# V caches loaded in 32 KB runs with a lag of three steps, no closing barrier, and a smaller last load, in a decode kernel with cached attention

## Chip, cores, metric

One core of a Trainium2 chip. The metric is the device time of the kernel in microseconds (us), median of several executions. TensorE is called PE, VectorE DVE, ScalarE ACT; SP is the engine that issues the loads. A load has landed when the last of the 16 DMA engines that share it has reported. Its forerunner is the load ahead of it in the queue. The lead of a load is the time from its issue to the landing of its forerunner.

## The reference

One token goes through a transformer block: layer norm and modulation, attention over a cache of 65,536 keys (32 query heads, 4 KV heads, head size 128), output projection, layer norm again, and a gated GELU feed-forward layer (1024 to 3584 to 1024).

```python
mod = (_silu(c) @ w_mod).reshape(c.shape[0], 6, 1, -1)      # six vectors sa, ca, ga, sb, cb, gb
h = _layernorm(x) * (1 + ca) + sa
q = (h @ wq) per head;  k, v = k_cache, v_cache repeated 8 times
p = _softmax(q k^T * Dh ** -0.5);  o = p v
x = x + ga * (o @ wo)
h = _layernorm(x) * (1 + cb) + sb
x = x + gb * ((_gelu(h @ w_gate) * (h @ w_up)) @ w_down)
```

K and V are 67.1 MB each, the weights 51.4 MB: 185.6 MB are read for one token. The rest of the work is small.

## The kernel before

The caches are cut into NC = 32 chunks of 8192 keys: 2 MB of K and 2 MB of V each, 64 keys (16 KB) on each of the 128 partitions. SBUF holds ten slots of 2 MB. K uses slots 0 to 3 and comes in pairs of chunks (4 MB, 32 KB a partition); V uses slots 4 to 7 and comes chunk by chunk (2 MB, 16 KB a partition).

```python
SITES = 4
KU = 2
# ... planning: the order of the queue of loads
for i in range(NC + 2):
    if i < NC and i % KU == 0:
        j_k[i] = plan_load(kv_src(kh, i, KU), flat(KU * CH, DH), i % SITES, kfill[i % SITES // KU], KU)
    if i >= 2:
        j = i - 2
        j_v[j] = plan_load(kv_src(vh, j), flat(CH, DH), SITES + j % SITES, vfill[j % SITES])
# ... then the weights: wo (4 loads), gate (4), up (4), down (3 of 2 MB, then 2 of 512 KB)
```

SP issues the loads strictly in this order. Each waits until PE has finished with what lay in its slots:

```python
def issue_ready():
    while issued[0] < len(loads):
        j = loads[issued[0]]
        if any(q.freed is None for q in j.prev):
            return
        SP.wait(*(q.freed for q in j.prev))
        sp.dma_start(j.view, j.src).then_inc(j.tok[0], 16)
        issued[0] += 1
```

PE works in steps. Step i transposes K chunk i (T), multiplies Q by K chunk i-1 (QK) and P by V chunk i-2 (PV), interleaved in quarters. MT and MB are small matmuls for the maxima of the scores. DVE and ACT copy the transposes out, take the maxima and make the exponentials.

```python
def PV(q):
    j = i - 2
    # ...
    if q == 0:
        pwait(vfill[s], j, it)      # V has landed
        pwait(ex[s], j, it)         # its exponentials are made
    # ... 16 matmuls with V as the stationary operand
    if q == NB - 1:
        release(j_v[j], pt[("PV", j)])

T(0); QK(0); T(1); QK(1); PV(0); T(2); QK(2); QK(3); PV(1); T(3); PV(2); MT(); PV(3); MB()   # shown on one line
```

Steps 0 to 3 are written out; steps 4 to 31 are a loop of four steps in PE's program; steps 32 to 34 and all that follows are written out again. Everything stands in a block whose end is a barrier of all engines:

```python
with nc.Block() as block:
    @block.sync
    def _(sp_unused):
        emit_all()
```

## Time and profile before

443.58 us (443.48 to 443.66, three runs).

| read from the profile | value |
|---|---|
| span of the profiled execution | 441.8 us (its time: 443.68) |
| PE busy | 333.3 us, 75% |
| DMA, mean over the span | 421 GB/s |
| K pair (4 MB), landing to landing, median | 9.67 us |
| V chunk (2 MB), landing to landing, median | 4.85 us |
| last landing; end of span | 438.37; 441.80 us |

The last V chunk was issued at 344.54 and the load ahead of it landed at 361.04, so SP was 16.5 us early.

### The profile page before, as it was taken

The numbers are of one execution on the slowest core, as the hardware profiler recorded it, in microseconds if no ns is written. First come the engines' busy times: TensorE is split into PE (matmuls) and PEld (weight loads), VectorE is DVE, ScalarE is ACT, GpSimd is POOL, SyncE is SP. The second block draws the span as 40 slices with busy tenths as digits, with TensorE's granted clock in tenths as the row PEclk, the third lists the DMA queues.
The fourth block names the chain that finished last, engine by engine and source line by source line (L and its number), as shares of the span: only waits on it lengthen the run. The fifth ranks groups of instructions, "written<-read, shape, count | busy, mean of one in ns | idle before, by whom it ended". The sixth has DMA issues, their size and how long they took to land.

```text
span 441.8 us, 16747 instructions
## 1 busy us (share of the span) xinstructions
PE 333.3 (75%) x7849; PEld 323.6 (73%) x7849; DVE 164.9 (37%) x282; ACT 142.9 (32%) x548; POOL 3.7 (1%) x21
## 2 busy tenths in 40 slices
PE   1333428889998987988898899979998797367534
PEld 1332427879988987988898899879998796367434
DVE  1000006534645564365446336534545343401000
ACT  1000003643434563435246343524643344200000
POOL 2000000000000000000000000000000000000000
PEclk9999999965968998599669759956969758555555
DMA  8999999999999999999999999999999999999994
GB/s 330 425 426 426 449 429 418 444 412 436 427 423 444 418 445 416 442 433 424 438 426 447 421 438 425 433 442 421 437 423 445 426 429 429 422 424 425 424 425 182
DMA packets 13088, 186.08 MB, mean 421 GB/s; under 512 B 1280, under 2 KB 1280, under 8 KB 3584
## 3 DMA queue, kind: packets, MB, share of 16 engines
q1 hardware_dynamic: 13024, 185.60, 98.4%
q8 instruction: 25, 0.41, 0.3%
q14 instruction: 7, 0.06, 0.0%
q10 hardware_dynamic: 32, 0.00, 0.0%
HBM read 185.60 MB, written 0.00 MB: 420 GB/s over the span
## 4 chain that ended last, share of the span: by engine, by line
DMA 53%; PE 40%; issue 3%; ACT 2%; DVE 1%; SPq 1%
DMA slots<-in_A_v_cache_dram 27%; PE kt_ps L419 22%; DMA slots<-in_A_k_cache_dram 9%; PE b L483 8%; PE sc_ps L439 7%; DMA slots<-in_B_w_up_dram 6%; DMA slots<-in_B_w_down_dram 6%; DMA slots<-in_w_mod_dram 5%; PE b L463 2%; ACT p_sb L549 1%; SPq L216 1%; ACT kt_sb L518 1%; PE b L453 1%; PE kt_ps L318 0%; DVE kt_sb L518 0%
## 5 line engine op out<-in xcount | busy, mean ns | idle before, releaser
L419 PE MATMUL kt_ps<-ident,slots 128*128 128x128 bf16 x2048 | 171.4, 251 | 18.7 <-DMA slots<-in_A_k_cache_dram 15.9
L419 PEld LDWEIGHTS kt_ps<-ident,slots 128*128 128x128 bf16 x2048 | 147.8, 114 | 20.5 <-issue 10.2
L518 DVE COPY kt_sb<-kt_ps 128x2048 bf16<-128x2048 bf16 x96 | 117.5, 1224 | 108.2 <-PE kt_ps L419 108.0
L518 ACT ACTIVATE kt_sb<-kt_ps 128x2048 bf16<-128x2048 bf16 x32 | 60.1, 1877 | 224.7 <-PE kt_ps L419 224.7
L483 PE MATMUL b<-p_sb,slots 128*128 128x8 bf16 x2048 | 70.4, 167 | 22.2 <-DMA slots<-in_A_v_cache_dram 9.6
L549 ACT ACTIVATE p_sb<-sc_ps,mneg 128x64 bf16<-128x64 f32 x256 | 83.5, 561 | 5.0 <-DVE mneg L544 5.0
L483 PEld LDWEIGHTS b<-p_sb,slots 128*128 128x128 bf16 x2048 | 64.7, 99 | 24.8 <-issue 13.5
L549 ACT ACTIVATION_READ_ACCUMULATOR p_sb<-sc_ps,mneg 128x1 f32 x256 | 77.1, 366 | 0.0
L439 PE MATMUL sc_ps<-q_buf,kt_sb 128*128 128x8 bf16 x2048 | 67.4, 167 | 1.1 <-issue 1.1
L439 PEld LDWEIGHTS sc_ps<-q_buf,kt_sb 128*128 128x128 bf16 x2048 | 65.3, 100 | 1.2 <-issue 1.1
L537 DVE TENSOR_REDUCE m_col<-sc_ps 128x8 f32<-128x512 f32 x32 | 21.8, 681 | 5.2 <-PE sc_ps L439 5.2
L318 PE MATMUL kt_ps<-h_col,slots 128*128 128x1 bf16 x448 | 16.0, 172 | 10.0 <-DMA slots<-in_B_w_up_dram 7.0
L318 PE MATMUL sc_ps<-s_col,slots 128*128 128x1 bf16 x384 | 11.5, 165 | 15.8 <-DMA slots<-in_w_mod_dram 15.8
L318 PEld LDWEIGHTS kt_ps<-h_col,slots 128*128 128x128 bf16 x448 | 15.5, 118 | 10.5 <-DMA slots<-in_B_w_up_dram 7.4
L318 PEld LDWEIGHTS sc_ps<-s_col,slots 128*128 128x128 bf16 x384 | 11.1, 105 | 16.4 <-DMA slots<-in_w_mod_dram 16.4
L542 DVE TENSOR_REDUCE mg<-b 8x1 f32<-8x128 f32 x32 | 8.9, 279 | 32.5 <-PE b L453 32.5
L318 PE MATMUL sc_ps<-h_col,slots 128*128 128x1 bf16 x256 | 7.4, 165 | 12.6 <-DMA slots<-in_A_wq_dram 12.6
L318 PEld LDWEIGHTS sc_ps<-h_col,slots 128*128 128x128 bf16 x256 | 7.1, 104 | 12.9 <-DMA slots<-in_A_wq_dram 9.3
L463 PE MATMUL b<-negi,mg 8*128 8x8 f32 x64 | 14.3, 294 | 0.4 <-DVE mg L542 0.4
L318 PE MATMUL kt_ps<-u_col,slots 128*128 128x1 bf16 x224 | 6.6, 165 | 9.3 <-DMA slots<-in_B_w_down_dram 9.3
L463 PEld LDWEIGHTS b<-negi,mg 8*128 8x128 f32 x64 | 11.4, 220 | 2.7 <-DVE mg L542 0.6
L318 PEld LDWEIGHTS kt_ps<-u_col,slots 128*128 128x128 bf16 x224 | 6.3, 104 | 9.6 <-DMA slots<-in_B_w_down_dram 6.4
(74 smaller groups left out, 62.5 us busy)
## 6 DMA issues: line engine op xcount, KB each, us to landing
slots<-in_A_k_cache_dram SPq DMA_DIRECT2D x16, 4096.0 KB, 19.4
slots<-in_A_v_cache_dram SPq DMA_DIRECT2D x32, 2048.0 KB, 26.7
slots<-in_w_mod_dram SPq DMA_DIRECT2D x8, 1536.0 KB, 19.0
slots<-in_A_wq_dram SPq DMA_DIRECT2D x4, 2048.0 KB, 37.1
slots<-in_A_wo_dram SPq DMA_DIRECT2D x4, 2048.0 KB, 33.1
slots<-in_B_w_gate_dram SPq DMA_DIRECT2D x4, 1792.0 KB, 30.0
slots<-in_B_w_up_dram SPq DMA_DIRECT2D x4, 1792.0 KB, 28.9
slots<-in_B_w_down_dram SPq DMA_DIRECT2D x3, 2048.0 KB, 30.3
```

Of the source, the lines that this page charges most:

```text
L216: sp.dma_start(j.view, j.src).then_inc(j.tok[0], 16)
L318: ins = pe.matmul(bank[:, j:j + 1], w, rhs[:, k0 + kk:k0 + kk + 1], start=first, stop=True, skip_group_check=True,)
L419: ins = pe.transpose(kt_ps[:, half * 2048 + t * P:half * 2048 + (t + 1) * P], j_k[i - i % KU].view[:, i % KU * CH + b * TB + t, :], ident[ ...
L439: ins = pe.matmul(sc_ps[:, base + n * REP:base + (n + 1) * REP], kt_sb[:, j % 2, n, :], q_buf[:, j % SITES, :], start=True, stop=True,)
L453: ins = pe.transpose(b6[0:REP, 32:32 + P], m_col[:, j % 2, :], identf[:, :]) if emit else None
L463: ins = pe.matmul(b6[:, 256:256 + REP], mg8[:, j % 2:j % 2 + 1].to_broadcast([REP, P]), negi[:, :], start=True, stop=True,)
L483: ins = pe.matmul(b7[:, s * REP:(s + 1) * REP], j_v[j].view[:, n, :], p_sb[:, s, n, :], start=(n == 0), stop=(n == CH - 1),)
L518: ev[i % SITES][b].done(act.activation(dst, src, ACT.Copy) if E_ is AC else dve.tensor_copy(dst, src))
L537: m1[s].done(dve.tensor_reduce(m_col[:, j % 2, :].unsqueeze(2), scv, AX.X, ALU.max))
L542: m2[s].done(dve.tensor_reduce(mg8[:, j % 2:j % 2 + 1], b6[0:REP, 32:32 + P], AX.X, ALU.max))
L549: ins = act.activation(p_sb[:, s, :, h], scv[:, h, :], ACT.Exp, bias=mneg[:, j, h:h + 1], scale=scale, accum_out=z_all[:, j, h:h + 1],)
```

## The change

The intent: V, like K, in runs of 32 KB a partition, so half as many packets; hence two V buffers of 4 MB instead of four of 2 MB. PV is put a third step behind T, so that PE does not stand waiting for a pair. The closing barrier goes, since SP waits for the output anyway. The last down load is halved, so that fewer matmuls follow the last landing.

The core of the diff (renamings and formatting cut):

```diff
-KU = 2
+UN = 2
+LAG = 3
@@ load planning @@
-        for i in range(NC + 2):
-            if i < NC and i % KU == 0:
-                j_k[i] = plan_load(kv_src(kh, i, KU), ...)
-            if i >= 2:
-                j = i - 2
-                j_v[j] = plan_load(kv_src(vh, j), flat(CH, DH), SITES + j % SITES, vfill[j % SITES])
+        for i in range(0, NC + UN, UN):
+            if i < NC:
+                j_k[i] = plan_load(kv_src(kh, i, UN), ...)
+            if i >= UN:
+                j = i - UN
+                j_v[j] = plan_load(
+                    kv_src(vh, j, UN), flat(UN * CH, DH), SITES + j % SITES, vfill[j % SITES // UN], UN)
@@ last block of w_down @@
-            for e in range(0, UE, 2):
-                jb = plan_load(wd_v[:, b, e:e + 2, :], flat(2, D), next(tail))
+            for e, ne in ((0, 2), (2, 1), (3, 1)):
+                jb = plan_load(wd_v[:, b, e:e + ne, :], flat(ne, D), next(tail))
@@ QK @@
+                if b == 0 and j >= 2:
+                    pwait(ex[(j - 2) % SITES], j - 2, it)
@@ PV @@
-                j = i - 2
+                j = i - LAG
-                    pwait(vfill[s], j, it)
-                    pwait(ex[s], j, it)
+                    if j % UN == 0:
+                        pwait(vfill[s // UN], j, it)
+                    if i > NC:
+                        pwait(ex[s], j, it)
-                    release(j_v[j], pt[("PV", j)])
+                    release(j_v[j - j % UN], pt[("PV", j)], j % UN)
@@ end @@
-    with nc.Block() as block:
-
-        @block.sync
-        def _(sp_unused):
-            emit_all()
-
+    emit_all()
```

(The cut parts let each half of a pair be freed by itself. A load is issued when both halves of what lay there before are free.)

More of the change, by code (lines that the diff above doesn't have):

```diff
@@ L182, in bass_adaLN_cond__gqa_block_cached__geglu_ffn__decode_kernel @@
     nfill = [0] * NSLOT
-    kfill = [Site(nc, f"kfill{i}", 16) for i in range(SITES // KU)]
-    vfill = [Site(nc, f"vfill{i}", 16) for i in range(SITES)]
+    kfill = [Site(nc, f"kfill{i}", 16) for i in range(SITES // UN)]
+    vfill = [Site(nc, f"vfill{i}", 16) for i in range(SITES // UN)]
     last_job = [None] * NSLOT
@@ L197, in plan_load @@
         job.src = src
-        job.freed = None
+        job.freed = [None] * nslot
         job.prev = []
-        for t in range(slot, slot + nslot):
-            if last_job[t] is not None and last_job[t] not in job.prev:
-                job.prev.append(last_job[t])
-            last_job[t] = job
+        for t in range(nslot):
+            if last_job[slot + t] is not None:
+                job.prev.append(last_job[slot + t])
+            last_job[slot + t] = (job, t)
         loads.append(job)
@@ L212, in issue_ready @@
             j = loads[issued[0]]
-            if any(q.freed is None for q in j.prev):
+            if any(q.freed[t] is None for q, t in j.prev):
                 return
-            SP.wait(*(q.freed for q in j.prev))
+            SP.wait(*(q.freed[t] for q, t in j.prev))
             sp.dma_start(j.view, j.src).then_inc(j.tok[0], 16)
@@ L219, in bass_adaLN_cond__gqa_block_cached__geglu_ffn__decode_kernel, with release @@
     in_loop = [False]
-    def release(job, tok):
-        job.freed = tok
+    def release(job, tok, part=0):
+        job.freed[part] = tok
         if not in_loop[0]:
@@ L249, in emit_all @@
         j_k, j_v = {}, {}
-        for i in range(NC + 2):
-            if i < NC and i % KU == 0:
-                j_k[i] = plan_load(kv_src(kh, i, KU), flat(KU * CH, DH), i % SITES, kfill[i % SITES // KU], KU)
-            if i >= 2:
-                j = i - 2
-                j_v[j] = plan_load(kv_src(vh, j), flat(CH, DH), SITES + j % SITES, vfill[j % SITES])
+        for i in range(0, NC + UN, UN):
+            if i < NC:
+                j_k[i] = plan_load(kv_src(kh, i, UN), flat(UN * CH, DH), i % SITES, kfill[i % SITES // UN], UN)
+            if i >= UN:
+                j = i - UN
+                j_v[j] = plan_load(
+                    kv_src(vh, j, UN), flat(UN * CH, DH), SITES + j % SITES, vfill[j % SITES // UN], UN)
         tail = iter([8, 9, 0, 1, 2, 4, 3, 5, 6, 7, 8, 9] + [0, 1, 2, 4, 3, 5, 6, 7])
@@ L271, in emit_all @@
         while b < NBF:
-            for e in range(0, UE, 2):
-                jb = plan_load(wd_v[:, b, e:e + 2, :], flat(2, D), next(tail))
-                j_d.append((jb, jb.view, b * UE + e, 2))
+            for e, ne in ((0, 2), (2, 1), (3, 1)):
+                jb = plan_load(wd_v[:, b, e:e + ne, :], flat(ne, D), next(tail))
+                j_d.append((jb, jb.view, b * UE + e, ne))
             b += 1
@@ L409, in T @@
                 s, half = i % SITES, b % 2
-                if b == 0 and i % KU == 0:
-                    pwait(kfill[s // KU], i, it)
+                if b == 0 and i % UN == 0:
+                    pwait(kfill[s // UN], i, it)
                 if b >= 2:
@@ L420, in T @@
                             kt_ps[:, half * 2048 + t * P:half * 2048 + (t + 1) * P],
-                            j_k[i - i % KU].view[:, i % KU * CH + b * TB + t, :],
+                            j_k[i - i % UN].view[:, i % UN * CH + b * TB + t, :],
                             ident[:, :],
@@ L424, in T @@
                 pt[("T", i, b)] = PE.done(ins)
-                if b == NB - 1 and i % KU == KU - 1:
-                    release(j_k[i - i % KU], pt[("T", i, b)])
+                if b == NB - 1:
+                    release(j_k[i - i % UN], pt[("T", i, b)], i % UN)
             def QK(b):
@@ L483, in PV @@
                         ins = pe.matmul(
-                            b7[:, s * REP:(s + 1) * REP], j_v[j].view[:, n, :], p_sb[:, s, n, :],
+                            b7[:, s * REP:(s + 1) * REP], j_v[j - j % UN].view[:, j % UN * CH + n, :], p_sb[:, s, n, :],
                             start=(n == 0), stop=(n == CH - 1),
@@ L520, in OC @@
             def OC():
-                j = i - 3
+                j = i - LAG - 1
                 if not 0 <= j < NC:
@@ L577, in emit_all @@
         mode[0] = "emit"
-        for i in range(LAST, NC + 3):
+        for i in range(LAST, NC + LAG + 1):
             pe_step(i)
```

## The prediction

> **What bounds the kernel now.** The DMA engines. The slices show them at 9 tenths or more from the second to the last but one; the page gives 421 GB/s on average. The trace's packets leave no idle time: from about 10 to 430 us at least 16 are always in flight, one for each engine. The Trainium skill ("DMA: Bandwidth & Descriptors", "Where 436 GB/s comes from") puts the ceiling at 435.2 GB/s; K at 9.67 us for 4 MB (landing to landing, from the DMA issues) is 434 GB/s, so this trace agrees. PE is busy 75% and waits: for K 15.9 us, for V 9.6 us, for P's exponentials 3.6 us plus 9 us "issue" (table of waits). Its clock is halved about half the time; a step takes 7.7 us at full and 10.3 to 11.2 us at half clock, against 9.7 us of loads. Reissues come 7 to 12 us before the queue would run dry. So PE's waits cost nothing, and the lag of three gains nothing by itself.
>
> **What the change does.**
> 1. V packets of 32 KB, not 16 KB. A 32 KB packet takes 1213 ns, a 16 KB packet 611 ns, so about 9 ns of each is fixed. Each engine sheds 128 packets: 1.15 us; 16 fewer loads shed 16 completion packets of 9 ns: 0.15 us. On the critical path.
> 2. Closing barrier: from the end of the output's wait (441.42) to the end of the span (441.80): 0.4 us.
> 3. Last down load halved: 8 matmuls, not 16, after the last landing (27 ns apart): 0.2 us; 2 KB packets give back 0.1 us.
> 4. Lag of three: PE's V waits vanish (about 20 us idle), off the path. V buffers also come free later: a pair goes out after P times V of its odd chunk, a step later. By the step times of before, the slack of V loads falls from 16-25 us to 5-10 us in the loop: no starvation. But the last V pair has no K pair ahead of it: it is issued at the end of step 30, which starts as the last K pair lands, when only a 4 MB V pair (9.7 us) is left in the queue. At half clock (as step 30 ran before: P times V ended 11.2 us after the landing, 1.1 of it waiting for V) the issue comes about 10.3 us after that landing, the first packet 0.8 to 1 us later: a hole of 1.5 us. At full clock, none. I charge 0.5 us.
>
> Sum: -1.3 -0.4 -0.1 +0.5 = -1.3 us: 442.3 us, range 440.9 to 444.0. Chances: faster by over 2% 2%, within 2% 96%, slower 2%.
>
> **What would show it.** V pairs landing 9.6 to 9.7 us apart, as K. P times V no longer waiting for V or "issue"; more of PE's idle time before the K transposes, for K. DMA slices as full as before, except perhaps a dent near 355 to 358 us, with the last V load issued 12 us later than before (344.5). No barrier after the output lands.
>
> **What would make it wrong.** HBM gaining more from long runs than packet arithmetic says (the ceiling allows some 8 us over the whole stream). The halved clock falling so that late V releases starve the queue in the loop: 1 to 3 us each, seen as slices under 420 GB/s. Engines drifting apart: at the end the fastest finishes some 5 us before the slowest, apparently because instruction fetches of 0.93 us fall unevenly; the new buffers may change this either way.

## More of the kernel before

Lines of the page of the kernel before: span, PE's busy time; in 40 equal slices the clock granted to PE, the busy tenths of the DMA engines and the GB/s; two DMA queues (packets, MB, share of the 16 engines' time); and two groups of instructions (busy us, mean ns of one | idle time of the engine just before them, what ended most of it).

```profile
span 441.8 us, 16747 instructions
...
PE 333.3 (75%) x7849; PEld 323.6 (73%) x7849; DVE 164.9 (37%) x282; ACT 142.9 (32%) x548; POOL 3.7 (1%) x21
...
PEclk9999999965968998599669759956969758555555
DMA  8999999999999999999999999999999999999994
GB/s 330 425 426 426 449 429 418 444 412 436 427 423 444 418 445 416 442 433 424 438 426 447 421 438 425 433 442 421 437 423 445 426 429 429 422 424 425 424 425 182
...
q1 hardware_dynamic: 13024, 185.60, 98.4%
q8 instruction: 25, 0.41, 0.3%
...
L419 PE MATMUL kt_ps<-ident,slots 128*128 128x128 bf16 x2048 | 171.4, 251 | 18.7 <-DMA slots<-in_A_k_cache_dram 15.9
...
L483 PE MATMUL b<-p_sb,slots 128*128 128x8 bf16 x2048 | 70.4, 167 | 22.2 <-DMA slots<-in_A_v_cache_dram 9.6
```

The DMA row is what to read first. It says 9 from the second slice to the one before the last: the load queue, not PE, bounds this kernel, and GB/s hardly moves. Below it, PE is idle 18.7 us before K transposes and 22.2 us before PV, some of it because V has not landed. That is waiting of an engine that is not the bottleneck. The row of q8 is easy to pass over: 25 packets of 16 KB of program text go through the same 16 engines.

The issues of SP near the end of the caches (start, us until the last of the group, tensor):

```profile
325.61 0.33 SPq L216 DMA_DIRECT2D slots<-in_A_k_cache_dram  x1
325.98 18.89 SPq L216 DMA_DIRECT2D slots<-in_A_v_cache_dram  x4
344.91 1.86 SPq L216 DMA_DIRECT2D slots<-in_A_wo_dram  x4
366.78 6.57 SPq L216 DMA_DIRECT2D slots<-in_B_w_gate_dram  x4
```

The last four V loads are spread from 325.98 to 344.87.

Loads in windows of 5 us there (columns: busy us and instructions of PE, weight loads, DVE, ACT, POOL; then the granted PE clock, the DMA share and GB/s):

```profile
core 0: us, PE busy (x) PEld busy (x) DVE busy (x) ACT busy (x) POOL busy (x), PEclk, DMA share, GB/s
345.00:350.00 5.00, 3.50 (x60) 3.50 (x61) 1.49 (x4) 3.04 (x17) 0.00 (x0) 0.73 0.95 406
350.00:355.00 5.00, 3.86 (x92) 3.77 (x90) 2.36 (x3) 0.00 (x0) 0.00 (x0) 0.50 0.99 426
355.00:360.00 5.00, 5.00 (x69) 4.86 (x68) 1.02 (x3) 3.26 (x11) 0.00 (x0) 0.50 1.03 439
360.00:365.00 5.00, 5.00 (x103) 5.00 (x101) 2.83 (x4) 1.17 (x8) 0.00 (x0) 0.57 1.03 442
```

GB/s stays above 400 in all four, also where PE's clock is halved.

## The result

The kernel after: 444.76 us, median of six runs (443.64 to 445.39); before, on the same chip, 443.57 us (443.48 to 443.66, six runs). The ratio is 1.0025, 95% interval 1.0012 to 1.0038. (A ratio here is the mean time of one kernel's runs over that of the other's of the same rounds, so it is not quite the ratio of the medians.) The kernel got slower by 1.2 us, 0.25%. That is within 2%, the class to which the prediction gave 96%, and the interval shows that it is not noise; but 442.3 had been predicted, with a range up to 444.0. The spread is also larger: 1.75 us, where before has 0.18 on this chip (0.91 on the chip of the last four runs).

The same lines of the page, after:

```profile
span 443.5 us, 16706 instructions
...
PE 320.2 (72%) x7849; PEld 311.2 (70%) x7849; DVE 165.0 (37%) x282; ACT 142.7 (32%) x548; POOL 3.7 (1%) x21
...
PEclk9999999968886995988589696978969695555555
DMA  8999999999999999999999999999999899999995
GB/s 328 430 423 425 451 424 433 434 429 428 426 431 429 434 441 427 431 434 431 429 446 429 429 434 432 429 443 432 429 437 429 358 378 421 419 425 421 426 426 217
...
q1 hardware_dynamic: 10864, 185.60, 97.9%
q8 instruction: 25, 0.41, 0.3%
...
L421 PE MATMUL kt_ps<-ident,slots 128*128 128x128 bf16 x2048 | 162.3, 243 | 42.4 <-DMA slots<-in_A_k_cache_dram 36.7
...
L489 PE MATMUL b<-p_sb,slots 128*128 128x8 bf16 x2048 | 69.0, 167 | 3.6 <-issue 2.4
```

Two numbers moved as predicted: PE's idle time before PV fell from 22.2 to 3.6 us, and its wait for K rose from 15.9 to 36.7 us. But the row of GB/s has a dent, 358 and 378, in the slices from 344 to 366 us, and the DMA row an 8.

SP's issues at the end of the caches:

```profile
321.99 0.33 SPq L217 DMA_DIRECT2D slots<-in_A_k_cache_dram  x1
335.16 20.13 SPq L217 DMA_DIRECT2D slots<-in_A_v_cache_dram  x2
355.33 1.97 SPq L217 DMA_DIRECT2D slots<-in_A_wo_dram  x4
357.34 18.24 SPq L217 DMA_DIRECT2D slots<-in_B_w_gate_dram  x4
```

The group of V holds two issues now: 335.16 (chunks 28 and 29) and 354.96 (chunks 30 and 31). Windows of 5 us:

```profile
core 0: us, PE busy (x) PEld busy (x) DVE busy (x) ACT busy (x) POOL busy (x), PEclk, DMA share, GB/s
345.00:350.00 5.00, 4.23 (x62) 4.24 (x63) 1.47 (x3) 1.00 (x8) 0.00 (x0) 0.50 0.97 419
350.00:355.00 5.00, 5.00 (x138) 4.90 (x134) 3.15 (x4) 0.92 (x1) 0.00 (x0) 0.86 0.61 262
355.00:360.00 5.00, 5.00 (x133) 4.98 (x134) 3.35 (x5) 3.47 (x17) 0.00 (x0) 1.00 0.84 315
360.00:365.00 5.00, 5.00 (x166) 4.89 (x164) 1.88 (x6) 3.57 (x14) 0.00 (x0) 1.00 0.99 426
```

262 and 315 GB/s where before had 426 and 439, with PE fully busy: the loads stand waiting for PE. The chain of work that ended last shows it (start, us, what): the last quarter of PV, then SP's issue of the V pair, then the wo loads behind it in the queue.

```profile
354.55 0.40 PE b L489 x16
...
354.96 0.33 SPq L217
...
356.28 26.61 DMA slots<-in_A_wo_dram
```

The trace tells for each load when the last of its 16 engines had landed. Last V loads and last down loads (computed from the trace, us):

```
                              before                after
landing of V chunk 29         356.20                355.37  (pair 28, 29)
last V load issued            344.54                354.96
landing of V chunk 31         365.90  (+9.70)       367.04  (+11.67)
landing of down load 3        435.88                437.00
landing of down load 4        437.14  (+1.26)       439.44  (+2.44)
last landing                  438.37  (+1.22)       440.67  (+1.23)
end of the span               441.80  (+3.43)       443.54  (+2.87)
16 KB program fetch no. 25    438.5                 437.0
```

So the two profiled executions differ by these terms: -0.83 us up to chunk 29; +1.97 us at the last V pair; nothing from there to the third down load; +1.18 us at the fourth; nothing at the last; -0.56 us after the last landing. That makes +1.7 us of span. A run's time exceeds the span by 1.9 us before and by 1.3 us after, which takes off nearly 0.6 us: +1.2 us for these two executions, as for the medians.

Two places carry the loss. Why the first, and what is the second?

### The profile page after: what moved, and what is told of

The parts are those of the page before. It is cut to its first block, busy times and chain, and to the rows that moved or that the text cites. A ratio compares the mean times of both kernels' runs of the same rounds, so it can differ in the third digit from the quotient of the medians.

```text
span 443.5 us, 16706 instructions
## 1 busy us (share of the span) xinstructions
PE 320.2 (72%) x7849; PEld 311.2 (70%) x7849; DVE 165.0 (37%) x282; ACT 142.7 (32%) x548; POOL 3.7 (1%) x21
## 4 chain that ended last, share of the span: by engine, by line
DMA 61%; PE 35%; issue 2%; SPq 1%; ACT 0%; DVE 0%
DMA slots<-in_A_k_cache_dram 39%; PE kt_ps L421 21%; DMA slots<-in_B_w_up_dram 6%; PE sc_ps L443 6%; DMA slots<-in_A_wo_dram 6%; DMA slots<-in_B_w_down_dram 5%; PE b L489 5%; DMA slots<-in_w_mod_dram 5%; SPq L217 1%; PE b L467 1%; PE kt_ps L320 1%; ACT kt_sb L524 0%; PE b L457 0%; PE b L676 0%; DVE y_row L678 0%
## 5 line engine op out<-in xcount | busy, mean ns | idle before, releaser
L421 PE MATMUL kt_ps<-ident,slots 128*128 128x128 bf16 x2048 | 162.3, 243 | 42.4 <-DMA slots<-in_A_k_cache_dram 36.7
L421 PEld LDWEIGHTS kt_ps<-ident,slots 128*128 128x128 bf16 x2048 | 140.2, 110 | 44.3 <-DMA slots<-in_A_k_cache_dram 29.8
L489 PE MATMUL b<-p_sb,slots 128*128 128x8 bf16 x2048 | 69.0, 167 | 3.6 <-issue 2.4
L489 PEld LDWEIGHTS b<-p_sb,slots 128*128 128x128 bf16 x2048 | 62.9, 97 | 4.5 <-issue 2.5
L443 PEld LDWEIGHTS sc_ps<-q_buf,kt_sb 128*128 128x128 bf16 x2048 | 64.2, 98 | 1.7 <-issue 1.7
L320 PE MATMUL sc_ps<-s_col,slots 128*128 128x1 bf16 x384 | 11.5, 165 | 15.9 <-DMA slots<-in_w_mod_dram 15.9
L467 PE MATMUL b<-negi,mg 8*128 8x8 f32 x64 | 13.0, 272 | 0.7 <-DVE mg L548 0.7
L467 PEld LDWEIGHTS b<-negi,mg 8*128 8x128 f32 x64 | 10.0, 195 | 3.4 <-DVE mg L548 1.1
```

Source lines behind the costliest of these rows:

```text
L320: ins = pe.matmul(bank[:, j:j + 1], w, rhs[:, k0 + kk:k0 + kk + 1], start=first, stop=True, skip_group_check=True,)
L421: ins = pe.transpose(kt_ps[:, half * 2048 + t * P:half * 2048 + (t + 1) * P], j_k[i - i % UN].view[:, i % UN * CH + b * TB + t, :], ident[ ...
L443: ins = pe.matmul(sc_ps[:, base + n * REP:base + (n + 1) * REP], kt_sb[:, j % 2, n, :], q_buf[:, j % SITES, :], start=True, stop=True,)
L467: ins = pe.matmul(b6[:, 256:256 + REP], mg8[:, j % 2:j % 2 + 1].to_broadcast([REP, P]), negi[:, :], start=True, stop=True,)
L489: ins = pe.matmul(b7[:, s * REP:(s + 1) * REP], j_v[j - j % UN].view[:, j % UN * CH + n, :], p_sb[:, s, n, :], start=(n == 0), stop=(n == ...
```

## The experiments

Theory for the first place, **the hole**: the last V pair has no K pair ahead of it. With two buffers and a lag of three it is issued at the end of step 30, 0.4 us before the load ahead of it lands. It landed 12.08 us after its issue, 2.4 us more than the 9.67 us of its transfer. So, in this theory, a load must be issued some 2.4 us ahead of its forerunner's landing or the engines run dry; 2.4 - 0.4 = 2.0 us is what was lost. For the second place: a fetch of program text falls on the slowest engine just before its last packets. The rivals: the loss comes from splitting the down load, from the missing barrier, or from the lag as such.

In the tables that follow, "before" is the kernel before, run in the same rounds on the same chip. The runs were made in three sets of four, each on its own chip: v_split_last to down_512; hold_last_v to wo_first_barrier; pad_tail to small_down. Runs of different sets should be compared through their before. Many of the steps below are under 1 us, so the landings in the trace (one execution each) are given beside the times.

### v_split_last: the last V pair as two loads

```diff
+                if j == NC - UN:
+                    for jj in range(j, NC):
+                        j_v[jj] = plan_load(
+                            kv_src(vh, jj), flat(CH, DH), SITES + jj % SITES, Site(nc, f"vlast{jj % UN}", 16))
+                    continue
```

(and PV waits for and frees these two singly)

> The kernel after, but the last V pair (chunks 30 and 31) is loaded as two loads of 2 MB, each issued when its own half of the buffer is free, as before. Hole theory: the last V pair went out only 0.4 us before the load ahead of it had landed, and an idle queue needs 2.4 us from issue to landing on top of the transfer, so the slowest engine lost 2.0 us; split, the first half goes out a step earlier (near 342 us, not 355), its landing follows the one before by 4.8 to 4.9 us, no slice falls under 415 GB/s, and the time falls by about 2 us, to 442.5 to 443. Rival (end theory): the loss sits at the end, where the down load before the last two landed 2.4 us after its forerunner, not 1.3 us; then the time stays at 444 to 445.

442.80 us (442.69 to 443.22); before 443.27; ratio 0.9991 (0.9978 to 1.0004). Chunk 30 went out at 342.85 and landed 4.85 us after its forerunner, chunk 31 4.91 us after that. The hole is gone. The late landing at the end stayed (2.46 us), so that is a loss of its own, as this run alone shows.

### wo_first: two wo loads ahead of the last V pair

```diff
+                if j == NC - UN:
+                    j_o += [(plan_load(wo_v[:, k:k + 8, :], flat(8, D), next(tail)), k, 8) for k in (0, 8)]
                 j_v[j] = plan_load(kv_src(vh, j, UN), ...)
```

> The kernel after, with two of the four wo loads put ahead of the last V pair in the queue (their slots are long free). No load is added or split. Hole theory: those 4 MB keep the engines busy for 9.7 us while the last V pair waits for its buffer, so its landing follows the one before by 9.7 us and the time falls by about 2 us, to 442.5 to 443; attention ends some 4 us later than in the kernel after, but not after the last wo load has landed plus a few us, so that costs nothing. Rival (end theory): 444 to 445 as the kernel after.

442.87 us (442.78 to 442.95); ratio 0.9991 (0.9978 to 1.0004). The last V pair was still issued only at 354.07, hardly earlier than in the kernel after, but now 10.8 us ahead of the landing before it. Windows of 5 us:

```profile
core 0: us, PE busy (x) PEld busy (x) DVE busy (x) ACT busy (x) POOL busy (x), PEclk, DMA share, GB/s
...
350.00:355.00 5.00, 5.00 (x133) 4.89 (x130) 2.89 (x5) 1.81 (x2) 0.00 (x0) 1.00 0.93 400
355.00:360.00 5.00, 5.00 (x146) 5.00 (x144) 4.08 (x5) 2.58 (x17) 0.00 (x0) 1.00 0.99 426
```

400 and 426 GB/s where the kernel after had 262 and 315. The last V pair itself landed 11.1 us after its forerunner, not 9.7 as expected: on 15 engines it is 9.7 us, the slowest landed 1.4 us behind them. Program fetch no. 17 had just passed (368.1 us). It is the same delay that the kernel after took one load later. PE waits 10 us for V here, at no cost.

### v_16k: V in 16 KB runs, all else as after

```diff
-                j_v[j] = plan_load(kv_src(vh, j, UN), flat(UN * CH, DH), ..., vfill[j % SITES // UN], UN)
+                for jj in range(j, j + UN):
+                    j_v[jj] = plan_load(kv_src(vh, jj), flat(CH, DH), SITES + jj % SITES, vfill[jj % SITES])
```

> The kernel after, but V again in four buffers of 2 MB (16 KB a partition); lag of three, no closing barrier and the small last load stay. Hole theory: no hole, since chunk 30 goes out a step earlier than chunk 31, so 2 us less; but V packets of 16 KB cost the slowest engine about 0.8 to 1.2 us more; sum about 443.5 to 444, and the V slices are full. If the lag of three itself were the loss (rival), the time would stay at 444.5 or go above it.

443.38 us (443.14 to 443.52); ratio 1.0001 (0.9988 to 1.0013). The lag of three without paired V loads has no hole (chunk 31 was issued 3.9 us ahead of the landing before it). Against the two kernels above, which have no hole either, 16 KB runs cost 0.5 to 0.6 us, less than the 0.8 to 1.2 us expected. Their intervals against before overlap, but no run of this kernel was as fast as any of wo_first. That is what the long V runs are worth. The trace says the same: packets of one size start every 607 ns (16 KB) or 1209 to 1210 ns (32 KB) on an engine, so two short ones take about 4.8 ns longer than one long one; over 128 such pairs on each engine, 0.61 us.

### down_512: the last down load of 512 KB again

```diff
-            for e, ne in ((0, 2), (2, 1), (3, 1)):
+            for e, ne in ((0, 2), (2, 2)):
```

> The kernel after, but with the last down load of 512 KB, as before. End theory: the split of the last down load brings the late landing of the load before it (2.4 us, not 1.3 us, after its forerunner), so undone the time falls by about 1 us, to 443.7. Hole theory with fetch by chance: a program fetch of 0.9 us (16 KB packet on another queue) fell on the slowest engine at 437 us, just before its last packets; whether it does so here depends on where the fetch falls, so either 444.9 (0.1 us more work at the end, fetch still there) or about 443.8 (fetch elsewhere); the landing of the last V pair stays 11.5 to 12 us after its forerunner in both.

444.67 us (443.33 to 446.44, six runs); ratio 1.0028 (1.0009 to 1.0047). The fourth down load was as late as ever (2.75 us after the third), and program fetch no. 25 came at 436.5 us. So the split is not what delays it. The last V pair landed 11.62 us after its forerunner. This kernel serves as the control on that chip: taking the hole away is worth 1.8 to 1.9 us (about 0.1 us of it may be the last down load, which also differs), and the spread of 3 us shrinks to 0.5 us and less.

### hold_last_v: the hole made larger

The last V pair is also held until the last K transposes are done.

```diff
+            if j.hold is not None:
+                if j.hold not in pt:
+                    return
+                SP.wait(pt[j.hold])
```

(with hold = the last quarter of T of chunk 31, for the last V pair alone)

> The kernel after, but the last V pair is held back until the last K transposes are done (near 361.4 us in the trace of after, instead of 354.96): the hole made larger by some 6.4 us. Hole theory: idle time of the queue counts one for one here, because the wo, gate, up and down loads stand behind that load and nothing later is waiting for PE: its landing follows the one before by about 18 us, and the time is about 451 us. Rival (the tail has slack, PE sets the end): clearly less than 451.

450.98 us (449.75 to 453.19); before 443.51; ratio 1.0170 (1.0148 to 1.0191). That is 6.3 us more than the kernel after, each against its before (+7.5 and +1.2): one for one, as expected. Windows of 5 us:

```profile
core 0: us, PE busy (x) PEld busy (x) DVE busy (x) ACT busy (x) POOL busy (x), PEclk, DMA share, GB/s
...
350.00:355.00 5.00, 5.00 (x137) 5.00 (x135) 3.88 (x5) 0.00 (x0) 0.00 (x0) 0.86 0.97 419
355.00:360.00 5.00, 5.00 (x130) 4.88 (x128) 2.91 (x6) 4.27 (x17) 0.00 (x0) 1.00 0.06 26
360.00:365.00 5.00, 5.00 (x147) 4.88 (x144) 2.86 (x6) 2.04 (x4) 0.00 (x0) 1.00 0.35 105
```

26 and 105 GB/s with PE busy all the while. The profiled execution was the slowest of the five (453.19 us); its V pair was issued 5.2 us after its forerunner had landed, not 0.4 us before, so here the hole was 5.6 us larger. It landed 18.7 us after its forerunner; 15 engines did so after 17.1 us, and program fetch no. 17 (371.1 us) fell on the last. Chunk 29 had already landed 2.5 us later than in the kernel after. That loss was in the loop: V pairs 6, 7 and 8, 9 were issued only 3.9 and 2.7 us ahead and landed 10.15 and 11.45 us after their forerunners, and one slice of the page fell to 390 GB/s. The loop is the same as in the kernel after.

### v32_lag2: V in pairs, but a lag of two

```diff
-LAG = 3
+LAG = 2
-                    if i > NC:
-                        pwait(ex[s], j, it)
+                    pwait(ex[s], j, it)
```

> The kernel after with P times V two steps behind the K transposes, as before (and it waits for the exponentials of its own chunk again). Theory: the lag of three is what lets V come in pairs. With a lag of two, step 2m starts as K lands and then needs a V pair that lands 9.7 us later, so PE stands about 6 us in every even step: two steps take 3 (until the wait) + 7 (waiting) + 5 + 8 to 11 us, 23 to 26 us, against 19.4 us of loads; slowdown of the loop by a sixth to a third, 490 to 540 us in all. If instead buffers run far enough ahead that V is there in time, about 443 us, and without the hole at the last V pair (it is issued a step earlier).

444.21 us (442.31 to 445.05, four runs); ratio 1.0022 (1.0007 to 1.0037). The expectation of 490 us or more was wrong by far. Who waited for whom (us in total, times, longest us):

```profile
PEld b L488 <- DMA slots<-in_A_v_cache_dram: 23.5, 14, 3.9
PE b L488 <- DMA slots<-in_A_v_cache_dram: 22.3, 14, 3.8
...
PE kt_ps L421 <- DMA slots<-in_A_k_cache_dram: 7.9, 1, 7.9
```

PE did wait for V, 14 times, but at most 3.9 us, and no longer for K in the loop (its one wait of 7.9 us for K is that for the first pair). The expectation took step 2m to begin as its K lands. The delay carries over instead: step 12, for one, began 3.5 us after its K had landed, and by then the wait for V is short. The slack that PE had (36.7 us of waiting for K in the kernel after) pays for it. What becomes thin is the lead of the K loads over the landing before them, 3.8 to 7.9 us from issue to landing of the forerunner from chunk 6 on. The profiled execution was the fastest, 442.31 us. It had no hole at the last V pair (issued 5.2 us ahead, landed 9.67 us later) and no late down load (1.23 us). But the loop had two dents already, slices of 380 and 406 GB/s: K pairs 6, 7 and 8, 9, issued 5.2 and 4.3 us ahead, landed 9.87 and 10.27 us after their forerunners. Others with leads of 3.8 and 3.9 us landed on time (9.67 and 9.70), so the 2.4 us are no sharp threshold. Why the other three executions took 444.1 to 445.1 us was not profiled, so it is open; more such late K loads would fit.

### barrier_only: the kernel before without its barrier

```diff
-    with nc.Block() as block: ...
+    emit_all()
```

> The kernel before without its closing barrier, nothing else. From the two traces: 0.4 us inside the span (441.42 to 441.80) and, since a run's time exceeds its span by 1.9 us before and by 1.3 us after, some 0.5 us outside it: 442.4 us. What is also asked: the 25th fetch of program text (16 KB, on its own DMA queue) came at 438.5 us in the kernel before, just after the last down load had landed, and at 434.6 to 437.0 us in all four kernels without the barrier, just before their last loads, where it set the slowest engine back by 1.2 us. If leaving out the barrier is what brings the fetch forward, the gain is eaten: 443.5 us, with the down load of 512 KB before the last landing 2.4 us after its forerunner, not 1.3 us. If the lag or the tail of the loop brings it forward, the landing stays at 1.3 us and the time is 442.4.

442.73 us (442.59 to 442.76); before 443.51; ratio 0.9981 (0.9968 to 0.9995). The barrier is worth 0.8 us (0.9 expected): 0.4 inside the span (441.8 to 441.4) and the rest outside it. The fetch stayed after the last data packets (438.1 us; they ended at 437.97), the fourth down load landed 1.23 us after the third. So the barrier has nothing to do with the late landing.

### wo_first_barrier: the barrier put back where the fetch is early

```diff
-    emit_all()
+    with nc.Block() as block: ...
```

> Two wo loads ahead of the last V pair (442.9 us without the barrier), with the closing barrier put back. If the barrier's absence brings the late program fetch forward: the barrier costs 0.9 us and the fetch gives 1.2 us back, so 442.5 us, with the fetch after the last landing. If it does not: 443.8 us, with the fetch again just before the last landings.

444.02 us (443.75 to 444.45); ratio 1.0009 (0.9995 to 1.0023). That is 0.9 us more than wo_first, each against its before. The fetch came at 435.4 us and the fourth down load landed 2.79 us after the third. The barrier is ruled out from this side too. What is left: all seven kernels with a lag of three so far have the late landing, the three with a lag of two have not (before, barrier_only, v32_lag2).

### pad_tail, drop_tail, pad_head: the length of PE's program behind the loop

With a lag of three, one PV less stands ahead of PE's loop and one more behind it: 64 matmuls, each with its weight load. To test whether that is what brings the fetch forward, three kernels lengthen or shorten the program.

pad_tail is barrier_only (lag of two) with 64 matmuls added behind the loop, to no effect on the result:

```diff
+                if j == NC - 1 and q == 0:
+                    for n in range(CH):
+                        pe.matmul(b7[:, s * REP:(s + 1) * REP], j_v[j].view[:, n, :], p_sb[:, s, n, :],
+                                  start=(n == 0), stop=(n == CH - 1))
```

> The kernel before without its barrier (442.7 us, late fetch at 438.1 us), with the 64 matmuls of the last P times V made twice (same result, 1.7 to 3.4 us more PE work behind the loop, where PE has to wait for loads anyway). Program-length theory: a lag of three moves the 64 matmuls of one P times V from ahead of the loop to behind it, and that is what brings the 25th program fetch from after the last landing to before it; so here too it comes early (near 435 us) and delays the slowest engine by 1.2 us: 443.9 us, the next-to-last down load landing 2.4 to 2.7 us after its forerunner. Rival (it is the lag's timing, not the length of the program behind the loop): 442.7 to 442.9, fetch near 438 us.

443.67 us (443.35 to 444.32); before 443.52; ratio 1.0004 (0.9990 to 1.0017). Fetch at 435.9 us; the fourth down load 2.76 us after the third.

drop_tail is wo_first (lag of three) without 56 of the last 64 PV matmuls. It makes other numbers than the reference:

```diff
-                    for t in range(TB):
+                    for t in range(TB) if j < NC - 1 else (0, TB - 1):
```

> The kernel with two wo loads ahead of the last V pair, without 56 of the 64 matmuls of the last P times V: the result is wrong on purpose. Program-length theory: the tail is nearly as long as with a lag of two, so the 25th fetch comes after the last landing (near 438 us) and the time falls from 442.9 to about 441.7 us. Rival: the time stays at 442.8 (PE's work there is off the path) and the fetch near 435 us.

441.75 us (441.44 to 442.10); ratio 0.9961 (0.9948 to 0.9975). Fetch at 437.0 us, the fourth down load 1.22 us after the third, last landing at 437.27. The fetch did not wait for the last landing, as had been expected, but the last data packet had ended at 436.92, just ahead of it, so it delayed nothing. The dropped chunk is one of eight of the last KV head, and the difference stays within the tolerance. That says nothing for the kernel; it leaves out work and is no candidate.

pad_head is wo_first with 64 idle matmuls ahead of the loop:

```diff
+        for _ in range(64):
+            pe.matmul(b6[:, 448:448 + REP], ident[:, :], q_buf[:, 0, :], start=True, stop=True)
         for i in range(FIRST):
```

> The kernel with two wo loads ahead of the last V pair, with 64 idle matmuls ahead of the loop, so that the program ahead of the loop is as long as with a lag of two (and 128 instructions longer in all). If what counts is where the loop begins in the program, the fetch comes late: 441.7 us. If what counts is the length behind the loop, or the whole length, it stays early: 442.9 us, next-to-last down load 2.4 to 2.7 us after its forerunner. The 1.7 us of PE work fall while PE waits for K and cost nothing.

443.12 us (442.53 to 443.23); ratio 0.9987 (0.9974 to 1.0001). Fetch at 434.5 us, the fourth down load 2.59 us after the third: nothing moved.

The three agree. Adding 64 matmuls behind the loop brings the loss to a kernel with a lag of two (+0.9 us against barrier_only, each against its before); taking 56 away frees a kernel with a lag of three from it (-1.4 us against wo_first, each against its before); 64 matmuls ahead of the loop changed nothing that stands out of the noise. The intervals of pad_tail and barrier_only just overlap, but no run of pad_tail was as fast as any of barrier_only, and the late landing is there in one trace and not in the other. The work itself was off the path in all three, since PE waits for down loads at that time.

### small_down: the small last load where no fetch disturbs it

barrier_only with the three down loads of the change.

> The kernel before without its barrier (442.7 us), with the last down load of 256 KB: the split alone, where no late fetch disturbs it. 8 matmuls fewer after the last landing (0.2 us), 9 packets more on each engine (0.1 us): 442.6 us, within 0.2 us of the barrier's removal alone; the fetch stays after the last landing.

442.63 us (442.48 to 442.81); before 443.52; ratio 0.9980 (0.9966 to 0.9994). Against barrier_only 0.1 us, as expected. That is too small to be told from noise. This is the fastest kernel that does all the work, though only 0.1 us ahead of barrier_only and 0.4 to 0.5 us ahead of v_split_last and wo_first, each against its before.

## Why the prediction was wrong

**What bounds the kernel: right.** The loads do, before and after. PE's waiting moved from V to K and nothing came of it. In the loop, V was issued 8 to 12 us ahead of the landing before it (5 to 10 predicted), so the queue did not run dry there in the profiled execution. In the slow execution of hold_last_v, which has the same loop, it did at two V pairs (leads of 3.9 and 2.7 us, a slice of 390 GB/s): the prediction had named this under what would make it wrong.

**V in long runs: right sign, half the size.** Charged with -1.3 us, measured 0.5 to 0.6 us (v_16k against v_split_last and wo_first). The step that failed reads "about 9 ns of each is fixed". It was taken from the durations of packets, 1213 and 611 ns, but successive packets of an engine overlap by about 4 ns: the distance between starts is 1209 and 607 ns, and 4.8 ns is what a packet costs. Durations of overlapping things must not be added; the pitch is to be read.

**Closing barrier: right, and too small.** Charged with -0.4 us, measured 0.8 us (barrier_only). The span shows 0.4; the part behind the span was not seen, because only one kernel's difference of time and span was known.

**Last down load: right.** Charged with -0.1 us, measured 0.1 (small_down).

**The hole: right place, right cause, a quarter of the size.** The prediction named the load, the step and the dent near 355 us; the load was issued at 354.96. The terms that failed are "the first packet 0.8 to 1 us later: a hole of 1.5 us" and "I charge 0.5 us". The landing of the forerunner had been set against the first packet of the next load. The issue came 9.2 us after the K landing, and the first packet 0.96 us after the issue, as predicted; by the prediction's own sum that is a hole of 0.5 us, just what was charged. But it left out both ends: the last packets of the forerunner had ended 0.3 us before its landing, and the first packets into the dry queue took 1.5 to 2.0 us instead of 1.21. Landing must be compared with landing: here a load into a dry queue landed 2.4 us later than its transfer takes (12.08 us from issue; 12.02 in down_512). So the hole was 2.0 us even though step 30 had its full clock back after 351 us, and it does not vanish at full clock as easily as the prediction said. v_split_last, wo_first and hold_last_v show cause and size; removing it gave 1.8 to 1.9 us.

**The program fetch: not foreseen.** The prediction named instruction fetches only as something that "may change this either way" through the buffers. Program fetch no. 25 falls on an engine that is already among the last and sets it back by 1.2 us. The trace of the kernel after shows why this was not chance: fetches no. 17 to 24 had set back eight engines, and at the third down load these landed at 436.65 to 437.00 us, level, the other eight at 435.09 to 435.51. The next fetch fell on one of the late eight. In the kernel before it came just after the last packets; the lag of three lengthens PE's program behind the loop by 64 matmuls, and it comes before them. pad_tail, drop_tail and pad_head show that it is the length behind the loop and that it costs 0.9 to 1.4 us. The Trainium skill ("Runtime: NRT & Kernel Launch", "Instruction fetch mechanics") states that a sequencer fetches its program in blocks of 16 KB, one after the other, ahead of what it executes. Blocks of 16 KB are what the trace shows on that queue (25 packets of 16,384 bytes), and none came between 172 and 376 us in the kernel before, while PE repeated its loop. At which instruction a fetch is asked for, and why the program ahead of the loop does not count, no run here shows.

**The sum.** Measured: -0.6 (V) - 0.8 (barrier) - 0.1 (down) + 1.8 to 2.0 (hole) + 0.9 to 1.4 (fetch) = +1.2 to +1.9 us; the kernel measured +1.2. Both losses need one part of the change, the lag of three (the hole needs the pairs as well: v_16k has none), which had been written down as gaining nothing by itself. The errors in V (0.7 us too much) and in the barrier (0.4 us too little) partly cancel, by luck. It was right that the lag gains nothing. The lag costs, at the end of the loop, where a steady state ends, and that was charged too lightly.

Open: why the kernels with a hole spread over 1.75 to 3.4 us, and those without over 0.2 to 1.0 us (v32_lag2 apart, with 2.7). PE's clock changes between half and full in step 30, and the issue of the last V pair hangs on that step; that was not tested by itself. The loop is a second candidate: in the slowest execution of hold_last_v, two V pairs there landed 2.3 us late in all. Fast and slow executions of one kernel were not both profiled.

## What to carry to other kernels

When the load queue is the bottleneck, check at the end of every steady pattern whether the next load is issued early enough: compare its issue with the landing of its forerunner, and ask for more than the lead that a load into a dry queue shows (2.4 us here, beyond its transfer; two loads with leads of 3.9 and 4.3 us were still 0.5 to 0.6 us late). A load that must wait for a buffer should have others ahead of it in the queue whose buffers are free; reordering two loads was enough. When an explanation rests on averages, look at the slowest of the 16 engines: it alone decides when a load has landed, and something as small as one block of program text can set it back.

## What the Trainium skill lacked or had wrong

- "DMA: Bandwidth & Descriptors", "Anatomy of one DMA — SWDGE (gpsimd) path": its fixed cost of about 2.0 us is given for loads issued from GpSimd; for loads from the SP queue the page's latency table has only the first byte, about 0.6 us. Here a 4 MB load from SP into a dry queue landed 12.08 us after its issue, 2.4 us beyond the 9.67 us that it takes in a full queue.
- "DMA: Bandwidth & Descriptors", "Why small descriptors are slow": a fixed cost of about 3 cycles a packet, without a time. Here two 16 KB packets take about 4.8 ns longer than one of 32 KB, worth 0.6 us in 67 MB; whether that is the page's cost, no run shows.
- "Runtime: NRT & Kernel Launch", "Instruction fetch mechanics" calls the cost of crossing a 16 KB boundary mostly hidden. That may hold for the engine that executes; in a kernel bound by loads the cost is not always hidden: the block takes about 0.93 us of one DMA engine, and when that engine is among the last, the load lands 1.2 to 1.6 us later. In the kernel after, fetches no. 1, 9, 17 and 25 were followed by such a late landing (5.04 for 3.6 us, 11.00 for 9.7, 6.09 for 4.86, 2.44 for 1.26), as if every eighth fell on the same engine; no page has that.
- "CRC Debugging", "Comparing the Two Runs" puts the refills of program text on queue 14. Here the 16 KB blocks came on queue 8 (25 packets); on queue 14 the page of the kernel after counts 6 more, 0.05 MB in all.
- No page tells that an execution's time beyond the span depends on a barrier at the program's end: 1.9 us with it, 1.3 us without.
